# The norm before the first gate/up stage: three of its tiles on VectorE, its transposes queued behind two weight slabs, and two pieces of other work moved by one product

## The chip, the cores and the metric

The kernel runs on one core of one Trainium2 chip. The metric is the device time of one execution in microseconds (us), which is compared as a median over several executions. In the traces the clock of the core starts at its first instruction, and all positions in time below are microseconds from there. The engines are called PE (TensorE), PEld (TensorE's weight loads), DVE (VectorE), ACT (ScalarE), POOL (GpSimd) and SP (SyncE, which issues the DMAs here) in the profile.

## The reference

The program is two layers of attention (A) and two gated feed-forward layers (B), alternating, on 2048 tokens of width 1024, in bfloat16.

```python
x = A_x
x = x + _A_ref(_layernorm(x), A_wqkv, A_wo)          # layer 1
x = x + _B_ref(_layernorm(x), B_W_gate, B_W_up, B_W_down)
x = x + _A_ref(_layernorm(x), A_wqkv, A_wo)          # layer 2, same weights
x = x + _B_ref(_layernorm(x), B_W_gate, B_W_up, B_W_down)

def _A_ref(x, wqkv, wo):
    # 32 heads of 32. Query s sees keys s, s-2, ..., s-14: 8 places.
    ...   # logits = sum over d of q*k[place], softmax over 8 places, o = sum a*v
def _B_ref(x, W_gate, W_up, W_down):
    # W_gate and W_up are 1024 x 3584
    gate = x @ W_gate; up = x @ W_up
    return (relu(gate) * up) @ W_down
```

## The kernel before

The tokens are worked in blocks of 512 (4 tiles of 128). Two blocks are interleaved by hand: every piece of work is put on a list with a moment, the list is sorted, and the engines then get their work in about this order. So a change of one number moves work on several engines, and a scheduler may settle ties otherwise than the number suggests.

The part that matters is the start, up to about 250 us. TensorE works there through: Q and K of block 0 with reductions L between them; Q and K of block 1; V of blocks 1 and 2; the output projection (acc_wo) of block 0; V of block 3; and then the first gate/up stage (acc_g and acc_u, 28 pairs of 8 + 8 matmuls), into which the reduction L of block 1 is put. Behind it come block 2's projections (there the stage ends), and much of the same in turn, up to 1645 us.

Before the gate/up stage, the four tiles of x of block 0 must be normalised (after the output projection has been added to them) and transposed by DMA. The transposes (xn_b to xnT_b) sit in the same queue as the weight slabs (1 MB each).

```python
def ln_steps(n, which, early=False, dve=()):        # cut
    ...
    def stats(t):
        def f():
            ...
            if t in dve:                       # this tile on VectorE
                hold[t] = ln_dve_stats(xt)     # 2 x bn_stats, bn_aggr, add, then a POOL pow
                return
            nc.scalar.activation(xn, xt[:], ACT.Square, accum_out=sq)      # else on ScalarE
            nc.scalar.activation(xn, xt[:], ACT.Identity, accum_out=sx)
            ...
            nc.gpsimd.tensor_tensor(rstd, vpe, neg_half[:, 0:1], op=ALU.pow)
            ...
    def turn(t=None): ...                      # sp_dma(xnT[:, t], xn[:, t], transpose)

def ln2(n, ats, turn_at=None, dve=()):
    stats, apply, turn, hold = ln_steps(n, "b", False, dve)
    for t, a in enumerate(ats):
        ev.append((a, stats[t]))
        ev.append((a + 4.0, apply[t]))
        if turn_at is None:
            ev.append((a + 6.0, turn(t)))      # transpose of tile t
    ...

def slab_events(events):                       # cut
    # the ring has 5 slabs: slab i is queued when slab i - 5 has been used up
    ...
    events.append((ends[i - RING] + 0.3 if i >= RING else 0.1 * i, f))
```

VectorE's other work around it: for block 0, a product of q and k for each of 8 parts (128x4096, 2.3 us), which TensorE reduces to L one by one. For block 1, products of half the size but in float32, added up on VectorE to one sum s, so that TensorE reduces once. That is 16 products and 14 adds of 2.3 us each, and every product and add reads both inputs from SBUF.

```python
for c in range(KC):                                                # block 0
    ev.append((t_qk0 + GAP0 * (K_STEP[c] + 1.0), mults[c]))
    if c < KC - 2:
        ev.append((t_qk0 + GAP0 * (K_STEP[c] + 2.5), reds[c]))      # L, one part
...
ev.append((t_qk1 + 0.5 * GRP, reds[KC - 2]))
ev.append((t_qk1 + 1.5 * GRP, reds[KC - 1]))
ev.append((t_qk1 + 1.6 * GRP, lambda: softmax(0)))
ln1(2, 36.0, t_qk1 + 2.0, True, 5.0)
...
sums1, red1 = prod_sum_steps(1)                                    # block 1
spread(sums1[:5], t_qk1 + 50.0, 4.4)                               # before the norm
spread(sums1[5:], t_v3 + 5.0, 4.4)                                 # behind it
want_wo(0, t_v3, t_v3)
spread(wo_steps(0), t_wo0, 2 * GRP)
ln2(0, [t_wo0 + 2 * GRP * (t + 1) + 0.1 for t in range(TPB)], None, (2, 3))
...
ev.append((t_gu0 + 48.1, red1))                                    # L of block 1
ev.append((t_gu0 + 48.2, lambda: softmax(1)))
```

## Time and profile before

| | before |
|---|---|
| time, median | 1649.46 us (1647.43 to 1649.85, 3 runs) |
| span of the profiled run, mean granted TensorE clock | 1644.8 us, 0.997 |
| TensorE busy | 1617.0 us, 98% |
| longest waits of TensorE | 8.9 us at the start, 7.8 us at the first gate matmul |

TensorE is the bound, so only what TensorE waits for can be won. The table of waits of TensorE in the kernel before says what it waited for; its columns are the waiting engine, tile and line, what released it, and then the total, the number of waits and the longest one. (The page's own list of waits is by groups of instructions; this one is by pairs.)

```profile
PE tp L295 <- DVE xn_first L277: 8.9, 1, 8.9
PE acc_g L118 <- DMA xnT_b<-xn_b: 7.8, 1, 7.8
PE L L118 <- POOL kh L363: 2.0, 1, 2.0
...
PE L L118 <- DVE prod L391: 0.5, 1, 0.5
```

(The rest, 0.2 us, is left out.) The 7.8 us is the wait for the transposes of the norm. The timeline of TensorE shows it in place (start, duration, engine, line, operation, number of matmuls; in brackets the idle time just before and what ended it):

```profile
143.24 5.10 PE L118 MATMUL acc_v<-xnT_a,w_v 128*128 128x512 bf16 x22
156.15 3.57 PE L118 MATMUL acc_g<-xnT_b,w_g 128*128 128x512 bf16 x8 [7.80 <-DMA xnT_b<-xn_b]
159.51 2.54 PE L118 MATMUL acc_u<-xnT_b,w_u 128*128 128x512 bf16 x8
```

The gap is paid twice: eight matmuls of a group take 1.73 us at full rate, start to start, but the first two groups behind the gap took from 156.15 to 161.88, 5.73 us instead of 3.45. (The last matmul of a group ends a little into the next group, so durations in such lines are 0.16 us longer than the steps.) The table by stretches has a granted clock of 0.50 from 155.0 to 160.6. The Trainium skill (TensorE: Matmul & The Clock Gate, "Why this matters for your kernels") says that idle gaps over about 3 us bring TensorE back to half its clock; this trace agrees, with 7.8 us.

The timeline of the DMA queue says why the transposes were late. Its durations are the time to issue, not to move:

```profile
138.90 6.56 SPq L107 DMA_TRANSPOSE xnT_b<-xn_b  x2
145.56 0.53 SPq L107 DMA_DIRECT2D w_u<-in_B_W_up_dram  x1
146.18 0.59 SPq L107 DMA_DIRECT2D w_g<-in_B_W_gate_dram  x1
146.86 7.15 SPq L107 DMA_TRANSPOSE xnT_b<-xn_b  x2
```

Nothing was queued from 126.7 to 138.90, although the two slabs' places were free, because both slabs stand in the queue behind two transposes, whose tiles were late. Then both slabs went out ahead of the other two transposes, the first of which took 4.35 us to issue (the first two took 1.23). One reason why the tiles were late is seen in POOL's timeline and VectorE's of this kernel, one line of each (tile 0 on ScalarE waited for this power, and tile 1 stood behind it):

```profile
134.60 2.67 POOL L230 TENSOR_TENSOR st_b<-st_b,neg_half 128x1 f32<-128x1 f32 x1 [39.32 <-ACT st_b L229]
```
```profile
134.59 2.28 DVE L429 TENSOR_TENSOR ac<-ac,t 128x2048 f32<-128x2048 f32 x1
```

POOL's power of one number for each partition took 2.67 us beside the VectorE add, against 0.55 us in the three powers after it. The Trainium skill (SBUF — State Buffer, "Who interferes with whom") says that a VectorE instruction with both inputs in SBUF contends with GpSimd's reads of SBUF through a shared port, which it calls an exclusive lock. The trace agrees: the power ended at 137.27, 0.40 us after the add.

Last, block 1's sum had time to spare before: VectorE finished it at 199.82 and TensorE came to its reduction at 206.87.

```profile
197.53 2.29 DVE L429 TENSOR_TENSOR s<-ac,t 128x2048 bf16<-128x2048 f32 x1
```
```profile
206.87 0.62 PE L118 MATMUL L<-s,sel 128*32 128x512 bf16 x8
```

### The profile page before, as it was taken

What the parts mean: (1) busy time and instruction counts of PE and PEld (TensorE: products, weight loads), DVE (VectorE), ACT (ScalarE), POOL (GpSimd) and SP (SyncE); (2) the same over time, 40 slices, a digit from 0 to 9 for tenths busy, and PEclk for the clock granted to TensorE, in tenths of its full rate; (3) what the DMA queues carried; (4) which work ended last, traced back from release to release, by engine and by line L of the source; (5) the groups of instructions that cost most, each with busy time, mean ns of one, the idle gap of its engine ahead of it and who ended that gap; (6) DMA issues with size and microseconds to landing.
All of it is one profiled execution on the core that took longest, in us unless ns stands there. A gap on an engine that the chain in (4) does not pass through costs nothing.

```text
span 1644.8 us, 18587 instructions
## 1 busy us (share of the span) xinstructions
PE 1617.0 (98%) x7527; PEld 777.8 (47%) x7576; DVE 1059.5 (64%) x918; ACT 511.9 (31%) x1057; POOL 264.6 (16%) x220
## 2 busy tenths in 40 slices
PE   6998999999999999999999999999999999999999
PEld 3553445444554445444454444544445444444444
DVE  3699898977298845949369493794927948211211
ACT  6834412424241512315124151340513411131110
POOL 2321105301052102111052010520105100000000
PEclk9998999999999999999999999999999999999999
DMA  9458766755747475774747748567475774655442
GB/s 304 83 159 217 186 175 187 200 162 169 214 152 211 133 209 157 217 206 150 208 156 204 181 154 231 162 185 204 152 225 176 193 217 152 204 156 181 154 162 69
DMA packets 371222, 296.81 MB, mean 180 GB/s; under 512 B 142400, under 2 KB 351296, under 8 KB 370240
## 3 DMA queue, kind: packets, MB, share of 16 engines
q1 hardware_dynamic: 370848, 295.10, 62.5%
q8 instruction: 59, 0.97, 0.3%
q10 hardware_dynamic: 288, 0.52, 0.1%
q14 instruction: 27, 0.22, 0.0%
HBM read 256.77 MB, written 21.00 MB: 169 GB/s over the span
## 4 chain that ended last, share of the span: by engine, by line
PE 91%; DVE 3%; ACT 3%; DMA 1%; issue 1%; POOL 1%; ACTq 0%; SPq 0%; DVEq 0%; POOLq 0%
PE acc_g L118 24%; PE acc_u L118 24%; PE dacc L118 23%; PE acc_wo L118 6%; PE acc_k L118 5%; PE acc_q L118 5%; PE acc_v L118 4%; DVE pv L481 1%; DMA x<-in_A_x_dram 1%; DVE pv L482 1%; DVE t L417 1%; DMA xnT_b<-xn_b 1%; ACT xn_a L225 0%; ACT xn_a L226 0%; ACT xn_a L242 0%
## 5 line engine op out<-in xcount | busy, mean ns | idle before, releaser
L118 PE MATMUL acc_g<-xnT_b,w_g 128*128 128x512 bf16 x1792 | 425.1, 380 | 7.8 <-DMA xnT_b<-xn_b 7.8
L118 PE MATMUL acc_u<-xnT_b,w_u 128*128 128x512 bf16 x1792 | 424.0, 379 | 0.0
L118 PE MATMUL dacc<-w_d,hT 128*128 128x512 bf16 x1759 | 386.3, 379 | 1.7
L551 DVE TENSOR_TENSOR hT<-acc_u,r 128x512 bf16<-128x512 f32 x224 | 153.7, 688 | 314.5 <-PE acc_u L118 301.9
L550 ACT ACTIVATE r<-acc_g 128x512 bf16<-128x512 f32 x224 | 132.6, 594 | 701.5 <-PE acc_g L118 693.0
L118 PEld LDWEIGHTS <-w_g 128*128 128x128 bf16 x1792 | 175.1, 98 | 221.7 <-DMA xnT_b<-xn_b 8.3
L118 PEld LDWEIGHTS <-w_u 128*128 128x128 bf16 x1792 | 175.6, 98 | 212.1 <-issue 1.4
L118 PEld LDWEIGHTS <-hT 128*128 128x128 bf16 x1792 | 175.3, 98 | 211.4
L419 DVE TENSOR_TENSOR t<-q,k 128x2048 f32<-128x2048 bf16 x84 | 191.8, 2291 | 9.7 <-ACT k L358 7.0
L429 DVE TENSOR_TENSOR ac<-ac,t 128x2048 f32<-128x2048 f32 x84 | 191.9, 2284 | 0.4
L363 POOL COPY kh<-k 128x14 bf16<-128x14 bf16 x64 | 85.2, 1336 | 448.5 <-ACT k L358 448.5
L578 DVE TENSOR_TENSOR x<-dacc,x 128x512 bf16<-128x512 f32 x64 | 42.5, 688 | 164.6 <-PE dacc L118 164.6
L481 DVE TENSOR_TENSOR pv<-a,vhm 128x4096 bf16<-128x4096 bf16 x64 | 145.4, 2285 | 0.0
L230 POOL TENSOR_TENSOR st_b<-st_b,neg_half 128x1 f32<-128x1 f32 x30 | 62.7, 2095 | 325.1 <-ACT st_b L229 325.1
L118 PE MATMUL acc_wo<-w_o,oT 128*128 128x512 bf16 x496 | 111.1, 379 | 1.0 <-DVE x L526 0.2
L230 POOL TENSOR_TENSOR st_a<-st_a,neg_half 128x1 f32<-128x1 f32 x32 | 48.1, 1504 | 337.5 <-ACT st_a L229 337.5
L118 PEld LDWEIGHTS <-oT 128*128 128x128 bf16 x512 | 50.1, 98 | 60.7 <-issue 0.5
L482 DVE TENSOR_TENSOR pv<-pv 128x2048 bf16<-128x2048 bf16 x64 | 77.6, 1218 | 0.2
L362 POOL COPY k<-kh 128x14 bf16<-128x14 bf16 x48 | 63.7, 1327 | 60.2 <-DVE t L419 43.8
L225 ACT ACTIVATE xn_b<-x 128x1024 bf16<-128x1024 bf16 x30 | 31.3, 1045 | 94.0 <-DVE x L526 94.0
L354 ACT CAST q<-acc_q 128x512 bf16<-128x512 f32 x64 | 37.3, 583 | 68.5 <-PE acc_q L118 68.5
L319 ACT CAST vT<-acc_v 128x512 bf16<-128x512 f32 x64 | 36.8, 587 | 63.6 <-PE acc_v L118 63.6
(125 smaller groups left out, 1205.2 us busy)
## 6 DMA issues: line engine op xcount, KB each, us to landing
w_g<-in_B_W_gate_dram SPq DMA_DIRECT2D x56, 1024.0 KB, 6.7
w_u<-in_B_W_up_dram SPq DMA_DIRECT2D x56, 1024.0 KB, 5.4
w_d<-in_B_W_down_dram SPq DMA_DIRECT2D x48, 1024.0 KB, 5.7
w_o<-in_A_wo_dram SPq DMA_DIRECT2D x16, 1024.0 KB, 7.4
vhm<-v_d SPq DMA_DIRECT2D x32, 284.0 KB, 6.8
v_d<-vT SPq DMA_DIRECT2D x8, 1024.0 KB, 9.9
oT<-o_d SPq DMA_DIRECT2D x32, 256.0 KB, 4.4
w_d<-in_B_W_down_dram SPq DMA_DIRECT2D x16, 512.0 KB, 3.8
```

The source lines that it names most:

```text
L118: tail_pe[0] = nc.tensor.matmul(*args, **kwargs).ins
L230: nc.gpsimd.tensor_tensor(rstd, vpe, neg_half[:, 0:1], op=ALU.pow)
L354: nc.scalar.copy(q[:], acc[:])
L362: nc.gpsimd.tensor_copy(k[:, 0:HALO], khalo[n - 1][:, c, :])
L363: nc.gpsimd.tensor_copy(khalo[n][:, c, :], k[:, BLK:BLK + HALO])
L419: nc.vector.tensor_tensor(t[:], i0, i1, op=ALU.mult)
L429: nc.vector.tensor_tensor(o, ac[:], t[:], op=ALU.add)
L481: nc.vector.tensor_tensor(tt[:], a_bc, v_sh, op=ALU.mult)
L482: nc.vector.tensor_tensor(tt[:, 0:4], tt[:, 0:4], tt[:, 4:8], op=ALU.add)
L550: nc.scalar.activation(r[:], acc[:], ACT.Relu)
L551: nc.vector.tensor_tensor(hold["hT"][:, j, :], accs["u"][:], r[:], op=ALU.mult)
L578: nc.vector.tensor_tensor(xs, ac[t], xs, op=ALU.add)
```

## The change

The intent is to have xnT_b ready when TensorE asks for it. (1) The transposes are given a later moment, so that the two slabs whose places are free come first in the queue. (2) Tile 1 of the norm moves from ScalarE to VectorE. (3) To make room for it, one product of block 1 moves behind the norm: the sums are held one product sooner. (4) Apart from it, block 0's reductions on TensorE are held one product later (with the norm of block 2 moved a little), to take the 2.0 us wait at the first L.

```diff
             if turn_at is None:
-                ev.append((a + 6.0, turn(t)))
+                ev.append((ats[-1] + 1.0 + 1.3 * t, turn(t)))          # (1)
 ...
         if c < KC - 2:
-            ev.append((t_qk0 + GAP0 * (K_STEP[c] + 2.5), reds[c]))
+            ev.append((t_qk0 + GAP0 * min(K_STEP[c] + 3.5, 2 * KC - 0.4), reds[c]))   # (4)
 ...
-    ln1(2, 36.0, t_qk1 + 2.0, True, 5.0)
+    ln1(2, 38.0, t_qk1 + 2.0, True, 5.0)                              # (4)
 ...
-    spread(sums1[:5], t_qk1 + 50.0, 4.4)
-    spread(sums1[5:], t_v3 + 5.0, 4.4)
+    spread(sums1[:4], t_qk1 + 50.0, 4.4)                              # (3)
+    spread(sums1[4:], t_v3 + 5.0, 4.4)                                # (3)
 ...
-    ln2(0, [t_wo0 + 2 * GRP * (t + 1) + 0.1 for t in range(TPB)], None, (2, 3))
+    ln2(0, [t_wo0 + 2 * GRP * (t + 1) + 0.1 for t in range(TPB)], None, (1, 2, 3))   # (2)
```

The marks (1) to (4) are not in the diff; the text uses them from here on.

## The prediction

> **What bounds the kernel now.** TensorE: busy 1617.0 of 1644.8 us (98%, the page's first part), and 91% of the chain that ended last. The table of waits leaves little: 8.9 us at the start, 7.8 us before the first gate matmul (acc_g, for the transposes of xn_b), 2.0 and 0.5 us before reductions L of block 0; the rest about 1 us or less.
>
> **The gap at the first gate matmul (timeline).** The last V matmuls end at 148.34 us; acc_g starts at 156.15. The norm's tiles were late: ScalarE wrote tile 1 at 144.2, VectorE tiles 2 and 3 at 143.7 and 145.2. ScalarE's tile 0 waited 2.67 us for a POOL power that started together with a VectorE add. The DMA engines moved nothing from 135 to 140, yet two 1 MB slabs were issued at 145.56 and 146.18, between transposes 1 and 2; transpose 2 then took 4.35 us to issue and the last landed at 156.1. The gap also halved the granted clock (0.50 until 160.6): the first 16 matmuls took 5.90 us instead of 3.45. The Trainium skill (TensorE: Matmul & The Clock Gate, "Why this matters for your kernels") says gaps over about 3 us do this; this trace agrees. Whole cost: 7.8 + 2.45 = 10.2 us.
>
> **What the change does, from the compiled order.**
> 1. The slabs are queued before all four transposes. Their slots fall free with the output projection, 132-134 us; 2 MB at the 350 GB/s seen later should be through by about 140.
> 2. Tile 1 moves to VectorE (two statistics of 0.68, 0.6 of apply), off ScalarE (about 4.7 us). A multiply of block 1 moves behind the norm. I put the last tile at 141-142, the last transpose landed at 145-147, before TensorE asks (148). So the 7.8 us and the cold clock go.
> 3. Block 0's reductions come one product later; the 2.0 us wait is put down to POOL, but a product ended at 41.35, just then. ScalarE's copies remain late, so later reductions wait instead; I count 1 us, range 0 to 2.
>
> **What is given back.** VectorE is nearly full from 80 to 200 us. Block 1's products and sums (2.2-2.3 us each) must pass before its reduction on TensorE, after the 14th gate/up pair. Before, they ended at 199.8 and TensorE asked at 206.9: slack 7.1 us. Now TensorE would ask some 10 us earlier, while VectorE gains little. Stepping through the new order with the trace's durations (an estimate): 0.3 to 0.7 us at several up-matmuls waiting for hT, and 2.7 us before the reduction, 4 in all. Gate/up of block 0 ends at about 249, not 255.9. Nothing after that changes.
>
> **Prediction:** 1649.5 - 10.2 + 4 - 1 = **1642 us**, 80% range 1637.5 to 1646. Faster by over 2%: 0.01; within 2%: 0.98; slower: 0.01.
>
> **Right or wrong is shown by:** acc_g's wait for xnT_b gone or under 1 us, granted clock 1.0 from 145 to 165; w_u and w_g issued about 132-135; transposes issued from about 137, landed before 148; a new TensorE wait of 2-4 us for the sum of block 1 (VectorE L429) near 198-201; the wait before the first L near 0, smaller ones before later L.
>
> **What would make it wrong.** The transposes crawl behind the slabs and land after 149 (gain under 4). POOL's powers are blocked by VectorE again. oT, which depends on VectorE, lands no earlier, so the 1 us is lost. VectorE has more slack than I reckon (gain up to 12). The noise: three runs spread over 2.4 us.

## The result, and the profile after

| | before | after |
|---|---|---|
| time, median | 1648.78 us (1647.43 to 1649.85, 4 runs) | 1642.31 us (1641.79 to 1644.07, 4 runs) |
| ratio, 95% interval | | 0.9963, 0.9946 to 0.998 |
| span of the profiled run, clock | 1644.8 us, 0.997 | 1640.5 us, 1.000 |
| TensorE busy | 1617.0 us | 1617.3 us |

TensorE's table of waits of the changed kernel shows that the 7.8 us has gone, that the wait at the first L has gone, and what came instead:

```profile
PE tp L295 <- DVE xn_first L277: 9.1, 1, 9.1
PE L L118 <- DVE s L429: 1.9, 1, 1.9
PE L L118 <- DVE prod L391: 1.7, 2, 0.9
...
PE acc_u L118 <- ACT r L550: 1.0, 1, 1.0
PE acc_u L118 <- DVE hT L551: 0.7, 1, 0.7
PE acc_g L118 <- ACT r L550: 0.2, 1, 0.2
```

The first gate matmul starts at once behind V, at full rate, as TensorE's timeline shows:

```profile
143.31 6.42 PE L118 MATMUL acc_v<-xnT_a,w_v 128*128 128x512 bf16 x29
149.57 1.89 PE L118 MATMUL acc_g<-xnT_b,w_g 128*128 128x512 bf16 x8
151.30 1.89 PE L118 MATMUL acc_u<-xnT_b,w_u 128*128 128x512 bf16 x8
```

The DMA queue has the two slabs first, and then all four transposes in one piece:

```profile
134.22 0.37 SPq L107 DMA_DIRECT2D w_u<-in_B_W_up_dram  x1
135.95 0.42 SPq L107 DMA_DIRECT2D w_g<-in_B_W_gate_dram  x1
137.79 8.40 SPq L107 DMA_TRANSPOSE xnT_b<-xn_b  x4
```

POOL's power for the first tile found no multiply or add of VectorE beside it, and took 0.55 us:

```profile
135.61 0.55 POOL L230 TENSOR_TENSOR st_b<-st_b,neg_half 128x1 f32<-128x1 f32 x1 [39.21 <-ACT st_b L229]
```

The price is at the reduction of block 1's sum. VectorE ends it at 202.71. TensorE, which no longer lost 10 us before, comes to it at 200.47, can do the first half of the reduction, and waits 1.90 us for the second (VectorE's timeline, then TensorE's):

```profile
200.43 2.28 DVE L429 TENSOR_TENSOR s<-ac,t 128x2048 bf16<-128x2048 f32 x1
```
```profile
200.47 0.40 PE L118 MATMUL L<-s,sel 128*32 128x512 bf16 x4
202.76 0.40 PE L118 MATMUL L<-s,sel 128*32 128x512 bf16 x4 [1.90 <-DVE s L429]
203.09 1.90 PE L118 MATMUL acc_g<-xnT_b,w_g 128*128 128x512 bf16 x8
204.83 1.89 PE L118 MATMUL acc_u<-xnT_b,w_u 128*128 128x512 bf16 x8
206.56 1.89 PE L118 MATMUL acc_g<-xnT_b,w_g 128*128 128x512 bf16 x8
```

To see where the time went I cut the profiled execution at five starts on TensorE that both kernels have. The columns are differences of starts in TensorE's timeline, in us, for all kernels:

| kernel | first V to first Q | Q, K, V with L, to first acc_wo | acc_wo and V, to first acc_g | gate/up of block 0 with L | the rest |
|---|---|---|---|---|---|
| before | 13.81 | 91.07 | 36.15 | 99.63 | 1389.02 |
| after | 16.19 | 90.41 | 27.63 | 101.88 | 1389.05 |
| e1_queue_only | 15.24 | 90.68 | 30.29 | 98.20 | 1389.02 |
| e2_tiles_only | 15.12 | 90.14 | 33.98 | 99.00 | 1389.02 |
| e3_without_hold_of_L | 16.55 | 90.39 | 27.89 | 104.15 | 1389.03 |
| e4_without_hold_of_sums | 15.64 | 90.38 | 28.07 | 98.82 | 1389.05 |
| e5_sum_read_later | 15.34 | 90.42 | 27.63 | 99.73 | 1389.05 |
| e6_half_the_products | 16.00 | 90.37 | 27.63 | 98.13 | 1389.03 |
| e7_after_again | 15.47 | 90.39 | 27.63 | 103.50 | 1388.98 |
| e8_last_reductions_later | 15.19 | 90.24 | 28.51 | 104.88 | 1389.05 |
| e9_queue_and_tiles | 15.56 | 90.40 | 29.01 | 98.81 | 1389.07 |
| e10_queue_and_earlier_hold | 16.32 | 90.37 | 27.90 | 104.72 | 1389.05 |
| e11_best_so_far | 16.44 | 90.05 | 28.09 | 98.65 | 1389.03 |

The first column is the same 64 matmuls in every kernel; it varies from 13.8 to 16.6 us because the granted clock becomes full sooner or later after the start (at 14.03 us in the kernel before, at 20.19 us in the changed one). None of the four parts touches this stage. It may be most of the spread of 2.4 us between runs of one kernel, but that is not shown: the changed kernel's two profiles differ there by 0.72 us. The Trainium skill (TensorE: Matmul & The Clock Gate, Part 1) says that activity is judged in free-running windows and that the cold start varies from run to run; these two moments agree. I leave the column out below. In the other four the changed kernel differs by -0.66, -8.52, +2.25 and +0.03 us, together -6.9 us; the medians say -6.5 us. Everything happens before 250 us, and nothing in the remaining 1389 us changes.

The +2.25 us in gate/up has three parts: the cold clock that went, -2.3 us; four new waits, +3.88 us (1.90, 1.04, 0.69 and 0.25 in the timeline); and 0.65 us that no wait names. That is 0.16 us for each of the four: a wait is counted from the modelled end of the last matmul, which lies 0.16 us into the next group's time. From 163.38 to 165.96, for one, a group with a wait of 0.69 us took 2.58 us, and 1.73 and 0.69 make 2.42.

### The profile page after: what moved, and what is told of

It is laid out like the page before. It is cut to its first block, busy times and chain, and to the rows that moved or that the text cites. A ratio compares the mean times of both kernels' runs of the same rounds, so it can differ in the third digit from the quotient of the medians.

```text
span 1640.5 us, 18585 instructions
## 1 busy us (share of the span) xinstructions
PE 1617.3 (99%) x7527; PEld 777.7 (47%) x7576; DVE 1061.3 (65%) x923; ACT 508.1 (31%) x1047; POOL 268.0 (16%) x220
## 4 chain that ended last, share of the span: by engine, by line
PE 93%; DVE 3%; ACT 2%; DMA 1%; issue 1%; POOL 0%; SPq 0%; DVEq 0%; ACTq 0%
PE dacc L118 23%; PE acc_g L118 22%; PE acc_u L118 22%; PE acc_wo L118 7%; PE acc_v L118 6%; PE acc_k L118 6%; PE acc_q L118 6%; DVE t L417 1%; DVE ac L429 1%; DMA x<-in_A_x_dram 1%; DMA v_d<-vT 1%; ACT xn_a L225 0%; ACT xn_a L226 0%; DVE prod L391 0%; PE L L118 0%
## 5 line engine op out<-in xcount | busy, mean ns | idle before, releaser
L481 DVE TENSOR_TENSOR pv<-a,vhm 128x4096 bf16<-128x4096 bf16 x64 | 145.2, 2282 | 0.0
L362 POOL COPY k<-kh 128x14 bf16<-128x14 bf16 x48 | 70.2, 1463 | 65.4 <-DVE t L419 43.8
```

Source lines behind the costliest of these rows:

```text
L362: nc.gpsimd.tensor_copy(k[:, 0:HALO], khalo[n - 1][:, c, :])
L481: nc.vector.tensor_tensor(tt[:], a_bc, v_sh, op=ALU.mult)
```

## The experiments

Experiments e1 to e4 were run together, so were e5 to e8, and so were e9 to e11, each group on one chip with runs of the kernel before: 1648.13 us (9 runs), 1648.52 us (9 runs) and 1648.77 us (9 runs). All outputs were correct but that of e6.

| kernel | parts | time, median us | ratio to before | 95% interval |
|---|---|---|---|---|
| e1_queue_only | (1) | 1640.83 | 0.9958 | 0.9946 to 0.9971 |
| e2_tiles_only | (2) | 1645.22 | 0.9985 | 0.9972 to 0.9999 |
| e3_without_hold_of_L | (1)(2)(3) | 1644.33 | 0.9977 | 0.9965 to 0.999 |
| e4_without_hold_of_sums | (1)(2)(4) | 1639.12 | 0.9947 | 0.9935 to 0.996 |
| e5_sum_read_later | (1)(2)(3)(4), L of block 1 later | 1639.95 | 0.9947 | 0.9935 to 0.996 |
| e6_half_the_products | (1)(2)(3)(4), less VectorE work | 1637.6 | 0.9934 | 0.9919 to 0.995 |
| e7_after_again | (1)(2)(3)(4) | 1642.75 | 0.9965 | 0.9952 to 0.9977 |
| e8_last_reductions_later | e4, two L of block 0 later | 1644.72 | 0.9979 | 0.9966 to 0.9991 |
| e9_queue_and_tiles | (1)(2) | 1640.55 | 0.9951 | 0.9939 to 0.9964 |
| e10_queue_and_earlier_hold | (1)(3) | 1644.68 | 0.9972 | 0.9958 to 0.9986 |
| e11_best_so_far | e4, L of block 1 later | 1638.85 | 0.9941 | 0.9929 to 0.9954 |

My theory was that the order in the queue is the lever, (2) closes the rest, and the price is VectorE's load; the rivals were that the faster norm does it, or that the holds do.

### e1_queue_only: part (1) alone

```diff
-                ev.append((a + 6.0, turn(t)))
+                ev.append((ats[-1] + 1.0 + 1.3 * t, turn(t)))
```

> The kernel before with one line changed: the four transposes are queued behind the two slabs; two norm tiles stay on ScalarE, the sums and the reductions L are as before. Theory (queue order and tile lateness are separate costs, and VectorE's work on block 1 sets what is given back): ScalarE writes tile 1 at about the same time as before, so the last transpose is issued some 2 us before TensorE asks and the gap at the first gate matmul shrinks from 7.8 to about 1.5 to 2.5 us, too short for a cold clock; from the first output projection matmul to the first gate matmul about 29.5 us (36.15 before, 27.63 after); the gate/up stage of block 0 about 98 to 99 us, because VectorE has one norm tile less to do than in the changed kernel and so makes the reduction of block 1 wait less than 1.9 us. Total 6 to 8 us faster than before, so as good as the whole change. Rival (the third tile on VectorE is what matters): gap stays above 4 us and the clock goes cold; gain below 4 us.

Measured: 1640.83 us. This one line alone is as fast as the whole change, or a little faster. The gap shrank from 7.80 to 1.93 us, and the first groups behind it ran at full rate (151.28 to 153.00):

```profile
143.16 6.18 PE L118 MATMUL acc_v<-xnT_a,w_v 128*128 128x512 bf16 x27
151.28 1.89 PE L118 MATMUL acc_g<-xnT_b,w_g 128*128 128x512 bf16 x8 [1.93 <-DMA xnT_b<-xn_b]
153.00 1.89 PE L118 MATMUL acc_u<-xnT_b,w_u 128*128 128x512 bf16 x8
```

The tiles are no earlier than before (the last at 146.2, and POOL's power still takes 2.67 us); each transpose now took 1.2 to 1.6 us to issue. So most of the loss was not the norm, but the place in the queue. VectorE ended the sum at 199.0 and TensorE came at 200.58, so there was no wait for the sum either.

### e2_tiles_only: part (2) alone

```diff
-    ln2(0, [...], None, (2, 3))
+    ln2(0, [...], None, (1, 2, 3))
```

> The kernel before with three norm tiles on VectorE only; the slabs stay queued between transposes 1 and 2. Theory: transpose 2 is again stuck behind the two slabs, so the gap at the first gate matmul stays at about 4 to 6 us and the clock goes cold (granted 0.5 for some 4 to 5 us); from the first output projection matmul to the first gate matmul 32 to 34.5 us; total 2 to 4 us faster than before. Rival (tile lateness was the cause): gap below 1 us, total 6 us or more faster.

Measured: 1645.22 us, 2.9 us less than before. The power of POOL took 0.55 us, the first transpose was issued at 137.20, and yet the third still took 4.21 us to issue behind the slabs (143.99 and 144.62), the gap was 5.8 us and the clock was cold behind it.

```profile
154.38 3.54 PE L118 MATMUL acc_g<-xnT_b,w_g 128*128 128x512 bf16 x8 [5.80 <-issue]
```

(The profile names no releaser for this wait; the last transpose landed at 154.28.) Moving a tile alone does not get past the queue. But it made only the first two tiles earlier: the last was ready at 146.1, against 145.2 before. So e2 does not test a norm that is early throughout, and no run has (2) and (3) without (1).

### e3_without_hold_of_L: all but part (4)

```diff
-            ev.append((t_qk0 + GAP0 * min(K_STEP[c] + 3.5, 2 * KC - 0.4), reds[c]))
+            ev.append((t_qk0 + GAP0 * (K_STEP[c] + 2.5), reds[c]))
 ...
-    ln1(2, 38.0, t_qk1 + 2.0, True, 5.0)
+    ln1(2, 36.0, t_qk1 + 2.0, True, 5.0)
```

> The changed kernel with the hold of block 0's reductions (and the later start of the norm of block 2) undone. Theory: from the first q matmul to the first of block 1 back to about 34.4 us (32.75 in the changed kernel), from there to the output projection back to 56.7 (57.66), the rest as in the changed kernel (gap 0, gate/up about 102 us): 0.3 to 1 us slower than the changed kernel, 6 us faster than before. Rival (the hold is worth its whole 2 us): 1.5 us or more slower than the changed kernel.

Measured: 1644.33 us, about 2 us slower than the changed kernel, more than I had expected and in the rival's range, but not for the rival's reason. The stage that holds the reductions (second column of the table of stages) took 90.39 us, as with the hold (90.41); its two halves took 33.67 and 56.71 us, where I had expected 34.4 and 56.7. The loss lies later, in gate/up, and behind the same 1.90 us wait at L:

```profile
203.69 0.40 PE L118 MATMUL L<-s,sel 128*32 128x512 bf16 x4 [1.90 <-DVE s L429]
204.02 2.68 PE L118 MATMUL acc_g<-xnT_b,w_g 128*128 128x512 bf16 x8
206.50 2.84 PE L118 MATMUL acc_u<-xnT_b,w_u 128*128 128x512 bf16 x8
209.17 1.89 PE L118 MATMUL acc_g<-xnT_b,w_g 128*128 128x512 bf16 x8
```

From 204.02 to 209.17 are 5.15 us for two groups, where the changed kernel took 3.47 (203.09 to 206.56, above). The clock fell. I come back to this at e7, the changed kernel again, whose clock fell too. Against that one e3 is 0.27 us longer before the first gate matmul and 0.65 us longer in gate/up, so by these two profiles some 0.9 us are (4)'s own.

### e4_without_hold_of_sums: all but part (3)

```diff
-    spread(sums1[:4], t_qk1 + 50.0, 4.4)
-    spread(sums1[4:], t_v3 + 5.0, 4.4)
+    spread(sums1[:5], t_qk1 + 50.0, 4.4)
+    spread(sums1[5:], t_v3 + 5.0, 4.4)
```

> The changed kernel with the sums of block 1 as before (five products ahead of the norm, not four). Theory (VectorE's work is only moved; its end sets when the reduction of block 1 may start): two sums now stand inside the norm, the last tile and transpose come 3 to 4 us later, a gap of 1 to 2 us appears at the first gate matmul (projection to gate 28.5 to 30 us), but the wait of the reduction for the sum shrinks by as much; the end of gate/up within 0.7 us of the changed kernel, total gain over before 5.5 to 7 us. Rival (the hold of the sums is a gain of its own): 1.3 us or more slower than the changed kernel.

Measured: 1639.12 us, about 3 us faster than the changed kernel. Both the theory (no difference over 0.7 us) and the rival (slower, the gap returns) failed. The gap stayed closed (0.3 us), and the wait for the sum went: VectorE ended it at 199.61, and TensorE came at 199.28 for the first half (VectorE's timeline, then TensorE's):

```profile
197.33 2.28 DVE L429 TENSOR_TENSOR s<-ac,t 128x2048 bf16<-128x2048 f32 x1
```
```profile
199.28 0.78 PE L118 MATMUL L<-s,sel 128*32 128x512 bf16 x8
```

The busy times between 125 and 145 us, of the changed kernel and of e4 (columns: stretch and length, then busy time and number of instructions of PE, PEld, DVE, ACT and POOL, granted clock, DMA share and GB/s), say why the room that (3) makes is not needed:

```profile
125.00:145.00 20.00, 19.95 (x93) 9.08 (x93) 18.13 (x27) 7.33 (x15) 2.16 (x4) 1.00 1.06 272
```
```profile
125.00:145.00 20.00, 19.95 (x94) 9.04 (x94) 19.77 (x27) 7.48 (x15) 1.65 (x3) 1.00 1.03 260
```

VectorE idled 1.87 us of 20 in the changed kernel, in short holes between the steps of the norm, mostly waiting for POOL's power. In e4 an add of block 1 stood between the steps of the norm and it idled 0.23 us. Its last tile was ready at 146.2 instead of 144.4, still just in time.

### e5_sum_read_later: the changed kernel, with L of block 1 one pair later

```diff
-    ev.append((t_gu0 + 48.1, red1))
-    ev.append((t_gu0 + 48.2, lambda: softmax(1)))
+    ev.append((t_gu0 + 51.6, red1))
+    ev.append((t_gu0 + 51.7, lambda: softmax(1)))
```

> The changed kernel with only the reduction of block 1's sum and its softmax placed one gate/up pair later on TensorE. My theory: the 1.9 us that TensorE waited for the sum was a matter of where the question stands in TensorE's order; one pair is 3.45 us, more than the 1.9 us, so this wait goes, nothing else moves, the first gate/up stage takes about 100 us instead of 101.9 and the time falls by 1.5 to 2 us against the changed kernel of the same rounds. Rival: VectorE is late altogether, so that the wait only turns into waits of the up-matmuls for hT of the same sum; the time stays within 0.5 us of the changed kernel.

Measured: 1639.95 us, 2.8 us faster than the changed kernel of the same rounds (e7, 1642.75). The wait at L went, the others stayed as they were (1.0, 0.6 and 0.2), and the gate/up stage took 99.73 us. The theory holds for the wait. The gain is larger than the 1.9 us of the wait, and e7 says why.

### e6_half_the_products: less work for VectorE

```diff
-        return [mult(h, c) for h in range(2) for c in range(KC)], red
+        if n == 1:   # wrong result on purpose: drops products 1 to 6 of the second half
+            return [mult(0, c) for c in range(KC)] + [mult(1, 0), mult(1, KC - 1)], red
+        return [mult(h, c) for h in range(2) for c in range(KC)], red
```

with the adds of the products that are left out left out as well.

> The changed kernel, but six of the eight products (and their adds) of the second half of block 1's sum are left out, so the result is wrong on purpose; VectorE loses about 12 x 2.3 us = 27 us of work. My theory: all of the 3.85 us that TensorE waited in the first gate/up stage comes from VectorE's load, the 1.2 us put down to ScalarE's r as well, because ScalarE's relu is held up by a tile that VectorE frees late. Then all of these waits go, the stage takes about 97.3 us instead of 101.9, and the time is 3.5 to 4.6 us under the changed kernel. Rival: the waits for r belong to ScalarE; they stay at about 1.2 us and the stage at about 98.5 us.

Measured: 1637.6 us, 5.15 us under e7, more than my theory's 3.5 to 4.6 (the cold clock told of at e7 may be part of it). The waits for r went as well, though no ScalarE instruction was touched; so they were VectorE's. One wait stayed, 0.6 us for hT at 165.4 (VectorE is there at the first product of the second half, which e6 keeps). The stage took 98.13 us, where my theory had 97.3 and the rival 98.5; the waits decide for the theory, but not all of them went.

```profile
PE acc_u L118 <- DVE hT L553: 0.6, 1, 0.6
```

The changed kernel's trace shows the way from VectorE to r. A copy of 14 columns of k on POOL waited for a VectorE product, a power of the next norm stood behind it on POOL, and ScalarE stood 7.17 us for that power, with the relu that writes r behind it (POOL's timeline, then ScalarE's):

```profile
165.44 0.20 POOL L362 COPY k<-kh 128x14 bf16<-128x14 bf16 x1 [21.64 <-DVE ac L417]
```
```profile
166.17 0.29 ACT L232 ACTIVATE st_a<-st_a 128x1 f32<-128x1 f32 x1 [7.17 <-POOL st_a L230]
```

In e6 no such copy stands before that power, and ScalarE stood 1.56 us. In e4 the copy waited until 162.09 and ScalarE stood 5.21 us; there TensorE did not wait for r.

### e7_after_again: the changed kernel once more

No edit.

> The changed kernel itself, to have it in the same rounds. If the times are steady it comes to 1641 to 1644 us, 0.996 of the kernel before, and the version without the earlier hold of the sums, 1639.1 us in the last rounds, was really about 3 us faster. If it comes to 1639 to 1640, that difference was chance between groups of rounds.

Measured: 1642.75 us, so the difference to e4 and e5 is real. The profiled run shows more than a repetition: the same waits, to 0.1 us, and yet 103.50 us for the gate/up stage instead of 101.88.

```profile
201.64 0.40 PE L118 MATMUL L<-s,sel 128*32 128x512 bf16 x4 [1.90 <-DVE s L429]
201.97 2.88 PE L118 MATMUL acc_g<-xnT_b,w_g 128*128 128x512 bf16 x8
204.64 2.64 PE L118 MATMUL acc_u<-xnT_b,w_u 128*128 128x512 bf16 x8
207.12 1.89 PE L118 MATMUL acc_g<-xnT_b,w_g 128*128 128x512 bf16 x8
```
```profile
203.00:206.00 3.00, 3.00 (x9) 1.08 (x8) 2.14 (x2) 1.11 (x2) 0.00 (x0) 0.50 0.00 0
```

The same wait of 1.90 us, and then two groups in 5.15 us (201.97 to 207.12) instead of 3.47. The granted clock was 0.50 from 203 to 206. In four profiles of kernels with this wait (the changed kernel twice, e3, e10), the clock fell behind it in three, and each time the two groups took 5.15 us, 1.68 us more. In the run times it is less plain. Of e10's five runs, the two with a mean clock of 1.000 took 1642.73 and 1643.28 us, and the three with 0.999 took 1644.68 to 1645.32; but of e7's own runs the profiled one took 1642.79, and one with 1.000 took 1642.75. (The first column of the table of stages moves these times too.) So the wait for the sum costs 1.9 us, and in some executions 1.7 us more. The Trainium skill (TensorE: Matmul & The Clock Gate, "Why this matters for your kernels") has gaps over about 3 us as the danger; here 1.90 us was enough in three of four cases, and the wait of 1.93 us in e1 did not do it.

No run was made to see what decides it, but the kept traces tell. In all 13 of them, once the clock is full, the granted clock changes only at whole multiples of 3.41 us from that moment (in e7: full at 18.43, half at 202.75, full at 206.16). I cut each trace into such windows and added up how long TensorE was busy in each with full-width matmuls, that is with all but the reductions L, which use 32 of its 128 columns (128*32 in the lines). Among the windows that began at full clock, the clock fell at the end of every one with at most 1.19 us of them and of none with 1.41 us or more; there is none in between. In e7, e3 and e10 the whole wait lies in one window, which leaves 0.85, 0.97 and 0.86 us. In the first profile of the changed kernel a window ends at 201.1, within the wait (200.87 to 202.76), and the next keeps 1.41 us; in e1 it is 1.64 us. So what counts is where the wait falls among the windows, which shifts from run to run. This is read from the traces; no change was made to test it.

### e8_last_reductions_later: e4, with two reductions of block 0 one projection later

```diff
-            ev.append((t_qk0 + GAP0 * min(K_STEP[c] + 3.5, 2 * KC - 0.4), reds[c]))
+            ev.append((t_qk0 + GAP0 * (K_STEP[c] + 3.5), reds[c]))
 ...
-    ev.append((t_qk1 + 0.5 * GRP, reds[KC - 2]))
-    ev.append((t_qk1 + 1.5 * GRP, reds[KC - 1]))
-    ev.append((t_qk1 + 1.6 * GRP, lambda: softmax(0)))
+    ev.append((t_qk1 + 1.5 * GRP, reds[KC - 2]))
+    ev.append((t_qk1 + 2.5 * GRP, reds[KC - 1]))
+    ev.append((t_qk1 + 2.6 * GRP, lambda: softmax(0)))
```

> The version without the earlier hold of the sums, and on TensorE the reductions of products 5 and 7 of block 0 placed one projection later (softmax of block 0 stays right behind the last). In that version TensorE waited 0.85 us for product 5 and 0.88 us for product 7 and for nothing else there. My theory: one projection is 1.73 us, which covers both waits, while product 7 still ends at the same time and the last reduction starts no later than now; so the two waits go, the output projection starts 1.7 us sooner, and the time falls by 1 to 1.7 us against 1639.1 us. Rival: what ends last there is VectorE and the way of block 0's output through memory; then the output projection gets a new wait for oT of 1 to 2 us, and the time stays within 0.5 us of 1639.1 us.

Measured: 1644.72 us, 5.6 us slower than e4: worse than either theory. Both waits at L went, as I had said, and at once the output projection waited 1.54 us for oT, as the rival had said: the second column of the table of stages is 90.24 us against 90.38. So nothing is to be won there, because block 0's output is back from memory no sooner. The loss comes from elsewhere. The scheduler now gives ScalarE, VectorE and POOL another order around the start of gate/up, in which statistics of the next norm stand before a relu. POOL's timeline, ScalarE's and TensorE's in turn:

```profile
162.75 2.12 POOL L362 COPY k<-kh 128x14 bf16<-128x14 bf16 x1 [17.04 <-DVE ac L417]
164.83 3.19 POOL L230 TENSOR_TENSOR st_a<-st_a,neg_half 128x1 f32<-128x1 f32 x2
```
```profile
165.40 0.29 ACT L232 ACTIVATE st_a<-st_a 128x1 f32<-128x1 f32 x1 [7.57 <-POOL st_a L230]
```
```profile
169.92 3.57 PE L118 MATMUL acc_u<-xnT_b,w_u 128*128 128x512 bf16 x8 [4.65 <-ACT r L550]
```

On POOL a copy of 14 columns stood ahead of the powers. It waited until 162.75 for a product of VectorE, and then took 2.12 us beside VectorE's multiplies (0.19 us in e4), and the two powers took 3.19. ScalarE stood 7.57 us for the first power, the relu behind it was late, and TensorE waited 4.65 us and then ran on a cold clock (3.57 us for a group). The changed kernel has the same stall (7.17 us, at e6), but with one relu more ahead of it. So VectorE held up POOL here twice, by the data and by running beside it, as the power of tile 0 was held up before the change.

### e9_queue_and_tiles: parts (1) and (2) alone

```diff
-                ev.append((a + 6.0, turn(t)))
+                ev.append((ats[-1] + 1.0 + 1.3 * t, turn(t)))
 ...
-    ln2(0, [...], None, (2, 3))
+    ln2(0, [...], None, (1, 2, 3))
```

> The kernel before with the queue line and the three tiles on VectorE, neither of the two holds. My theory: the reductions of block 0 held one product later are worth nothing, because the output projection cannot start before block 0's output is back from memory; so this comes out like the version without the earlier hold of the sums (1639.1 us), within 0.7 us, with no wait at the first gate matmul and none for the sum of block 1. Rival, as I predicted: the hold is worth about 1 us, and this is at 1640 us or above.

Measured: 1640.55 us, where the rival was, not my theory: part (4) is worth something. Against e11 of the same rounds, which has (4), it is 1.7 us slower (e11's other difference changed nothing, see there); against e4 of other rounds, by the ratios to the kernel before, 0.7 us. Stage by stage, e4 with (4) is 0.02 us shorter up to the output projection and 0.94 us shorter from there to the first gate matmul, 0.55 us of it because TensorE waited 0.84 us there in e9 and 0.29 us in e4. What comes sooner in e4 is VectorE, and it is not by the reductions: softmax of block 0 starts on VectorE 38.64 us after the first Q in e4 and 38.66 us in e9. But in the middle of softmax VectorE waits for ScalarE's exponential, 3.74 us in e4 and 4.63 us in e9, and from there on it is 0.9 us ahead. ScalarE does this exponential behind the norm of block 2, which (4) moves as well. No run separates the two lines of (4).

### e10_queue_and_earlier_hold: parts (1) and (3) alone

```diff
-                ev.append((a + 6.0, turn(t)))
+                ev.append((ats[-1] + 1.0 + 1.3 * t, turn(t)))
 ...
-    spread(sums1[:5], t_qk1 + 50.0, 4.4)
-    spread(sums1[5:], t_v3 + 5.0, 4.4)
+    spread(sums1[:4], t_qk1 + 50.0, 4.4)
+    spread(sums1[4:], t_v3 + 5.0, 4.4)
```

> The kernel before with the queue line and the sums of block 1 held one product sooner; two tiles on VectorE, no hold of the reductions. My theory: the earlier hold takes one product (2.3 us) from before the norm, so the last tile comes earlier and the 1.9 us wait at the first gate matmul that the queue line alone left goes; but the product is paid behind the norm, the sum is ready 2 to 3 us later than with the queue line alone (199.0 us), and TensorE, which asks about 2 us sooner, waits 1.5 to 4 us for it. Time 1640.5 to 1643.5 us, no better than the queue line alone (1640.8). Rival: VectorE finds the time again, no wait for the sum, and it reaches 1638.5 to 1639.5 us.

Measured: 1644.68 us, 1.2 us slower than the slow end of my theory's range, and nowhere near the rival. The gap at the first gate matmul went, as expected; the waits that came with it were 1.9 us for the sum, 1.7 us for hT and 1.3 us for r, and the cold clock (1.7 us) came on top, which I had left out. So (3) does close the gap that (1) alone leaves, but at a price of more than it brings.

### e11_best_so_far: parts (1), (2) and (4), with L of block 1 one pair later

```diff
-    ev.append((t_gu0 + 48.1, red1))
-    ev.append((t_gu0 + 48.2, lambda: softmax(1)))
+    ev.append((t_gu0 + 51.6, red1))
+    ev.append((t_gu0 + 51.7, lambda: softmax(1)))
```

(on e4)

> The version without the earlier hold of the sums (1639.1 us), with the reduction of block 1's sum one gate/up pair later as well. In the profile of that version TensorE no longer waited for the sum, so my theory is that this changes nothing in the mean: 1639.1 us within 0.7, the first gate/up stage at 98.8 us. Rival: in other executions of that version the sum is sometimes late, and this one is 0.8 us or more faster with less spread.

Measured: 1638.85 us (1638.63 to 1639.14), ratio 0.9941. As my theory had it, the later L changes nothing in the mean where there was no wait; the spread is smaller (0.5 us against 1.6 in e4), but five runs do not show that this is more than chance. This is the best correct version: by the medians 3.5 us better than the changed kernel as first measured and 3.9 us better than e7, both of other rounds.

## Why the prediction was right

The predicted time (1642 us) was met (1642.31 us), and the class (within 2%) too. By points:

- **The gap and its cold clock, 10.2 us: right.** The stage before the first gate matmul is 8.5 us shorter (7.8 of them the wait), and the two groups behind it are 2.3 us shorter. I put it on the queue, the tiles and POOL together without weighing them. The experiments weigh them: (1) alone takes 5.9 of the 7.8 us and the cold clock, (2) alone takes 2.0 us of the gap and leaves the clock cold, (1) and (2) together leave 0.84 us.
- **The signs: mostly right.** No wait at acc_g, clock 1.00 from 145 to 165, slabs issued at 134.2 and 135.95, transposes from 137.8, the last landed at 148.11. Gate/up ended at 251.45; less the 2.4 us by which the first column was longer, that is the 249 I had. The slabs were slower than I said: I had them through by about 140, but they took 6.2 and 7.6 us from issue, so the second landed at about 143.6. My last tile at 141 to 142 came at 144.4, because I had not counted VectorE's waits for POOL's power (0.76 and 0.67 us) and the short holes between the small steps.
- **What is given back, 4 us: right in sum (4.5 us, without the cold clock that went), off in its parts.** I had 2.7 us at the reduction and 0.3 to 0.7 us at several up-matmuls for hT. It was 1.9 us at the reduction, one wait of 0.7 us for hT, 1.3 us for r, which I had not named, and 0.16 us more for each of these waits. e6 shows that those waits for r come from VectorE's load as well. And there is a term that I left out altogether: the clock falls behind the 1.9 us wait in some executions, which costs 1.7 us more. The profiled run was without it by luck of the windows (see e7), so that the sum fits this run so well is luck in part.
- **"While VectorE gains little": right for the changed kernel, but I took it for a cost of the whole change.** It is the cost of one part. Without (3), e4 has no wait for the sum, and with all of (3) but a later question, e5 has none either. I counted the product that moves behind the norm and did not ask whether the norm needed its room; e4 shows that it did not, and that the room was left empty in part.
- **The hold of block 0's reductions, 1 us (0 to 2): right in size, wrong in place.** I expected it at the reductions: the first wait did go and 0.85 and 0.89 us came at later ones, which is what I said. But e3, e4 and e9 all take 90.4 us to the output projection, so the 0.66 us by which the changed kernel is shorter there than the kernel before are not the hold's. What (4) brings, 0.7 to 1.7 us by e9 against e4 and e11, lies behind that, where VectorE is 0.9 us sooner after its wait for ScalarE (see e9).
- **"oT lands no earlier, so the 1 us is lost": half right.** e8 shows that the output projection cannot start sooner (it waited 1.54 us for oT at once). But the gain is not lost, it is at VectorE, by a way that I had not foreseen.

What stays open: which of the two lines of (4) brings its gain, whether an early norm without (1) would also close the gap, and whether e11's smaller spread is real.

## What to carry to other kernels

In a queue that is worked in order, look first at what stands before the late transfer: here one line that reordered the issues was worth as much as the whole change. When work is moved to make room, check that the room was needed, and who pays where the work lands; small steps that wait for another engine leave holes that other work could have filled. A short wait on TensorE can cost nearly twice its length when the clock falls behind it (1.9 us and 1.7 us more here), and whether it falls can change from run to run, so put the question (the reduction) a step later when nothing hurries it.

## What the Trainium skill lacked or had wrong

- TensorE: Matmul & The Clock Gate, "Why this matters for your kernels", has idle gaps over about 3 us as what brings the clock down. Here a wait of 1.90 us was followed by a granted clock of 0.50 in three of four profiles (1.68 us lost each time), while 1.93 us at another place (e1) was not. In these traces the clock fell behind a window of 3.41 us with at most 1.19 us of full-width matmuls, and never behind one with 1.41 us or more; the page has no such number.
- DMA: Bandwidth & Descriptors, "DMA Transpose (X-bar)", says what a transpose demands, but not that its issue slows down behind plain transfers in the same queue: a 128x1024 transpose took 1.23 us to issue alone, 4.35 us (before) and 4.21 us (e2) right behind two slabs of 1 MB, and up to 3.1 us in the changed kernel. The runs do not tell the slabs' place in the queue from their traffic as the cause.
- SBUF — State Buffer, "Who interferes with whom", agrees with what was seen (a power on POOL 0.55 us alone, 2.67 us beside a VectorE add with both inputs in SBUF). What it does not say is how far such a block reaches: in e8 a copy of 14 columns took 2.12 us instead of 0.19 and two powers took 3.19 us, behind a wait for VectorE's product, and ScalarE stood 7.57 us and TensorE 4.65 us for it.
